# Top-k attention with two expert layers: the scaled excess in fp32 instead of bf16

## The chip, the cores and the metric

The kernel runs on one core of a Trainium2 chip. The metric is the device time of one execution in microseconds; a time is the median of three runs. The engines are named as in the profile: PE (TensorE matmul), PEld (TensorE weight load), DVE (VectorE), ACT (ScalarE), POOL (GpSimd) and SP (SyncE).

## What is computed

Three layers follow one another. Attention keeps, in each row of scores, the 32 largest; a mixture of experts sends each token to one of eight; a dense layer with a hard-swish-like gate ends it.

```
scores = q @ k.T / 8                       # 2 batches, 8 heads, 576 x 576
kth    = 32nd largest of each row
attn   = softmax(scores where scores >= kth) @ v
x      = attn as 1152 tokens x 512
e      = argmax(x @ w_gate); x = gate * (relu(x @ w1[e]) @ w2[e])
h      = x @ w_in; out = (h * clip(h + 3, 0, 6) / 6) @ w_out
```

## The kernel before

The attention stage works on 72 units: 9 tiles of 128 rows times 8 heads, one unit being the 128 x 576 scores of a head for a tile. `in_steps` (L561) runs one step per unit and issues, in each step, pieces of several units that are at different depths. The order inside a step is the string `STEP = "RGLXSCVBTAZFMEQ"` (L36). Each engine works off its own queue in that order, and waits on semaphores for the others.

What happens to one unit, with the lines that matter:

- TensorE makes the scores (L321), ScalarE copies them to SBUF as fp32 (`fetch`, L326).
- **Round one** (L342, DVE): eight MAX8 instructions give the eight largest of each chunk of 72 columns.
- **Excess** (`excess`, L348, POOL): scores minus the eighth value of their chunk, the second operand being broadcast over the 72 columns of a chunk.
- **Cut** (`cut_excess`, L353, ACT): relu of that excess times 2**64, written to the tile `cut`.
- **Drop** (`drop_excess`, L356, POOL): scores minus `cut`, so that all that stood above the eighth value falls far down.
- **Round two** (L360, DVE): one MAX8 over the 576 columns that are left.
- **Merge** (L367, L369, L371, DVE): from the lists of chunk maxima the 32 largest in order.
- **Shift** (L385 on POOL for 200 columns, L390 on ACT for 376) and **below** (L394, ACT): the inputs of the transposes on TensorE (L408, L409), after which come the exponential (L415, ACT), the product with v (L426, PE) and the normalization (L432 to L434, DVE).

In step i POOL's queue holds the excess of unit i, the shift of unit i-3 and the drop of unit i-1, in this order; round two on DVE takes unit i-2, behind round one of unit i+1 and the merge of unit i-3. Every eighth step `judge` adds four small POOL instructions (L377 to L380). After four tiles, and again after eight, DVE also chooses the experts of the finished tiles (`route`, L456, with L466 `dl` and L491 `rd`), and POOL sends their rows with an indirect DMA (L140).

The expert layer and the dense layer come after the attention stage and run for the rest of the span, most of it matmuls.

Of the kernel before, what the change touches and what calls it, by code (L numbers as in the profile page):

```python
# [8 lines left out]
F32 = mybir.dt.float32  # L9
F32R = mybir.dt.float32r  # L10
BF = mybir.dt.bfloat16
# [7 lines left out]
P = 128  # L19
B, H, S, D = 2, 8, 576, 64  # L20
# [37 lines left out]
def topk_attention_moe_ffn_kernel(ctx, tc, qT, kT, vx, vT, wg, w1, w2, w_in, w_out, out, cap):  # L58
# [19 lines left out]
    def forward(fast):  # L78
# [112 lines left out]
        with ExitStack() as actx:  # L191
            big = actx.enter_context(tc.tile_pool(name=of + "big", bufs=1))
            wk = actx.enter_context(tc.tile_pool(name=of + "wk", bufs=2))
# [79 lines left out]
            for i in range(2):  # L273
                u = big.tile([P, 5 * P], F32, name=f"ub{i}")
# [19 lines left out]
            av, cuts = {}, {}  # L294
# [54 lines left out]
                                        op=OP.subtract)  # L349

            def cut_excess(u):
                cuts[u] = wk.tile([P, S], BF, name="cut")
                nc.scalar.activation(cuts[u], st2[u], AF.Relu, scale=PUSH)  # L353

            def drop_excess(u):
# [205 lines left out]
            def in_steps():  # L561
# [15 lines left out]
                def issue(u):  # L577
                    if u % 2 == 0:
                        if u % H == 0 and 2 < u // H + 2 < NT:
# [3 lines left out]
                routes = {}  # L583
                sent = 0
                blocks = {"X": (0, excess), "C": (1, cut_excess), "B": (1, drop_excess), "L": (2, round2), "S": (3, shift),
                          "Z": (3, shift_rest), "M": (3, below), "T": (4, ptr), "E": (4, expo), "A": (5, attv)}
                keep_warm(KW, wm)
# [434 lines left out]
```

## Time and profile before

| What | us |
|---|---|
| Median of three runs | 641.39 (641.07 to 641.99) |
| The profiled execution, its own time | 639.62 |
| Its span, first to last instruction | 637.8 |
| First to last drop (L356 starts) | 10.6 to 232.7 |
| Busy in the span: PE, DVE, ACT, POOL | 609.8, 375.5, 360.3, 311.3 |

The busy times are of the whole span. POOL, DVE and ACT do most of their work in the attention stage, up to about 235 us, and have little to do afterwards, so their shares of the span say little on the attention stage; the stretches of that stage have to be looked at by themselves. A record's duration includes a part that overlaps the next record on the same engine: on POOL some 40 ns.

### The profile page before, as it was taken

The numbers are of one execution on the slowest core, as the hardware profiler recorded it, in microseconds if no ns is written. First come the engines' busy times: TensorE is split into PE (matmuls) and PEld (weight loads), VectorE is DVE, ScalarE is ACT, GpSimd is POOL, SyncE is SP. The second block draws the span as 40 slices with busy tenths as digits, with TensorE's granted clock in tenths as the row PEclk, the third lists the DMA queues.
The fourth block names the chain that finished last, engine by engine and source line by source line (L and its number), as shares of the span: only waits on it lengthen the run. The fifth ranks groups of instructions, "written<-read, shape, count | busy, mean of one in ns | idle before, by whom it ended". The sixth has DMA issues, their size and how long they took to land.

```text
span 637.8 us, 12077 instructions
## 1 busy us (share of the span) xinstructions
PE 609.8 (96%) x4096; PEld 549.2 (86%) x4096; DVE 375.5 (59%) x1765; ACT 360.3 (56%) x687; POOL 311.3 (49%) x380
## 2 busy tenths in 40 slices
PE   8999999999888879999999999999999999999994
PEld 4888889888777767999999999999999999999993
DVE  5999999999999994002333323427665664222220
ACT  5999999989999963121334334336555553242221
POOL 7999999979999953001244222124234322030001
PEclk9999999999999979999999999999999999999998
DMA  8549600100000002885889887422222310020001
GB/s 268 168 134 386 212 17 2 35 2 18 18 18 19 2 1 95 293 290 148 306 264 280 276 308 239 165 64 85 81 85 84 97 34 1 1 99 1 1 1 54
DMA packets 36598, 74.13 MB, mean 116 GB/s; under 512 B 4016, under 2 KB 12464, under 8 KB 36528
## 3 DMA queue, kind: packets, MB, share of 16 engines
q1 hardware_dynamic: 34800, 68.55, 32.7%
q0 software_dynamic: 1728, 4.72, 2.0%
q8 instruction: 34, 0.56, 0.3%
q14 instruction: 36, 0.29, 0.2%
HBM read 63.83 MB, written 9.44 MB: 115 GB/s over the span
## 4 chain that ended last, share of the span: by engine, by line
PE 52%; DVE 24%; issue 15%; POOL 6%; ACT 1%; DMA 1%; DVEq 0%; SPq 0%; POOLq 0%; ACTq 0%
PE hps L819 13%; PE yps L819 13%; PE h L916 8%; PE acc L930 7%; DVE lists L342 7%; DVE lists L360 5%; DVE l L369 4%; DVE tops L371 3%; PE av L426 2%; POOL s L356 2%; PE ps L321 2%; PE pt L408 2%; POOL out_dram L939 1%; PE pt L566 1%; PE mix L443 1%
## 5 line engine op out<-in xcount | busy, mean ns | idle before, releaser
L342 DVE MAX8 lists<-s 128x8 f32<-128x72 f32 x576 | 118.6, 220 | 4.1 <-ACT s L326 4.1
L426 PE MATMUL av<-vt,pts 128*128 128x96 f32 (+1 forms) x800 | 100.5, 275 | 0.0
L916 PE MATMUL h<-x2h,fw 128*128 128x384 f32 x384 | 98.3, 336 | 0.9 <-DVE x2l L837 0.9
L426 PEld LDWEIGHTS av<-vt,pts 128*128 128x128 f32 (+1 forms) x800 | 92.1, 184 | 2.1 <-issue 0.9
L356 POOL TENSOR_TENSOR s<-s,cut 128x576 f32<-128x576 f32 x72 | 92.0, 1277 | 3.6 <-ACT cut L353 3.5
L819 PE MATMUL yps<-hT,wslot 128*128 128x192 f32 x512 | 90.9, 326 | 0.0
L930 PE MATMUL acc<-fw,gh 128*128 128x512 f32 x288 | 89.6, 392 | 0.0
L348 POOL TENSOR_TENSOR s<-s,lists 128x576 f32<-128x576 f32 x72 | 83.6, 1162 | 6.1 <-DVE lists L342 3.8
L408 PE MATMUL pt<-ident,ub 128*128 128x128 f32 x360 | 72.6, 287 | 13.5 <-POOL ub L385 7.9
L819 PE MATMUL hps<-xe,wslot 128*128 128x192 f32 x512 | 84.6, 326 | 0.2 <-DVE sc L184 0.2
L819 PEld LDWEIGHTS hps<-xe,wslot 128*128 128x128 f32 x512 | 83.4, 190 | 0.7 <-issue 0.7
L819 PEld LDWEIGHTS yps<-hT,wslot 128*128 128x128 f32 x512 | 82.1, 190 | 1.2
L408 PEld LDWEIGHTS pt<-ident,ub 128*128 128x128 f32 x360 | 50.8, 141 | 33.6 <-POOL ub L385 16.4
L916 PEld LDWEIGHTS h<-x2h,fw 128*128 128x128 f32 x384 | 70.5, 188 | 5.1 <-DVE x2l L837 1.2
L409 PE MATMUL pt<-drop,lb 128*128 128x128 bf16 x360 | 65.7, 220 | 0.0
L916 PE MATMUL h<-x2l,fw 128*128 128x384 f32 x192 | 64.7, 337 | 0.0
L930 PEld LDWEIGHTS acc<-fw,gh 128*128 128x128 f32 x288 | 53.4, 188 | 9.0
L919 ACT ACTIVATE g<-h,three 128x384 f32<-128x384 f32 x48 | 27.9, 581 | 55.7 <-PE h L916 55.7
L920 DVE SCALAR_TENSOR_TENSOR g<-g,h 128x384 f32<-128x384 f32 x48 | 26.5, 551 | 54.3 <-ACT g L919 53.9
L394 ACT ACTIVATE lb<-s,tops 128x576 bf16<-128x576 f32 x71 | 55.0, 775 | 4.9 <-DVE tops L371 2.8
L924 DVE TENSOR_TENSOR gl<-g,gh 128x384 fp32r<-128x384 f32 x48 | 27.4, 571 | 51.0 <-ACT gh L923 51.0
L923 ACT CAST gh<-g 128x384 fp32r<-128x384 f32 x48 | 24.7, 515 | 57.5 <-PE acc L930 52.9
(393 smaller groups left out, 1057.2 us busy)
## 6 DMA issues: line engine op xcount, KB each, us to landing
wslot<-in_w_dram SPq DMA_DIRECT2D x15, 2048.0 KB, 9.3
raw<-in_w_in_dram SPq DMA_DIRECT2D x16, 512.0 KB, 5.0
raw<-in_w_out_dram SPq DMA_DIRECT2D x16, 512.0 KB, 3.6
xs<-x_tok SPq DMA_DIRECT2D x8, 576.0 KB, 13.1
vt<-in_vx_dram SPq DMA_DIRECT2D x8, 365.0 KB, 3.6
kt<-in_kT_dram SPq DMA_DIRECT2D x8, 288.0 KB, 4.5
vts<-in_vT_dram SPq DMA_DIRECT2D x8, 288.0 KB, 3.8
qt<-in_qT_dram SPq DMA_DIRECT2D x9, 256.0 KB, 4.2
```

Source lines behind the costliest of these rows:

```text
L342: yield lambda c=c: nc.vector.max(lists[t % 2][:, h, c], st[u][:, c * CW:(c + 1) * CW])
L348: nc.gpsimd.tensor_tensor(s2, s, lists[t % 2][:, h, :NCK, KEEP:].to_broadcast([P, NCK, CW]), op=OP.subtract)
L356: nc.gpsimd.tensor_tensor(st2[u], st[u], cuts.pop(u), op=OP.subtract)
L360: nc.vector.max(lists[t % 2][:, h, NCK], st2.pop(u))
L394: nc.scalar.activation(lbufs[u % 2][:, :S], st.pop(u), AF.Relu, bias=tops[t][:, h, TOPK - 1:], scale=-1.0)
L408: nc.tensor.matmul(pt[:, c], ubufs[u % 2][:, cs], ident, is_transpose=True, start=True, stop=False)
L409: nc.tensor.matmul(pt[:, c], lbufs[u % 2][:, cs], drop, start=False, stop=True)
L426: nc.tensor.matmul(av[t, g][rows, h % 4], pts[:, c, cols], vt[b, h // 2][:, at:at + VC], start=c == 0, stop=c == 4)
L819: nc.tensor.matmul(out, wb[:, k], m[:, k], start=first and k == 0, stop=last and k == HP - 1)
L916: nc.tensor.matmul(h2, fw[f][:, 0, a, k * P:(k + 1) * P], (x2h, x2l)[b][:, k, c * CH:(c + 1) * CH], start=n == 0, stop=n == len(ops) - 1)
L919: nc.scalar.activation(g, h2, AF.Relu, bias=three)
L930: nc.tensor.matmul(acc[j], g[a][:, j * P:(j + 1) * P], fw[f][:, 1, b], start=f == 0 and n == 0, stop=f == NF - 1 and n == 2)
```

## The change

The tile `cut` is allocated in fp32 instead of bf16. ScalarE writes fp32 in L353, and POOL's subtraction in L356 reads two fp32 operands of 576 columns instead of one of fp32 and one of bf16. Both kernels hold the same instructions in the same order on every engine, with the same waits; the two buffers of `cut` take twice the space in SBUF.

```diff
             def cut_excess(u):
-                cuts[u] = wk.tile([P, S], BF, name="cut")
+                cuts[u] = wk.tile([P, S], F32, name="cut")
                 nc.scalar.activation(cuts[u], st2[u], AF.Relu, scale=PUSH)
```

## Rows read from the trace of the kernel before

**Rows 1.** Chain that ended last, shares of the span by engine (the page).

```profile
PE 52%; DVE 24%; issue 15%; POOL 6%; ACT 1%; DMA 1%; DVEq 0%; SPq 0%; POOLq 0%; ACTq 0%
```

**Rows 2.** Stretches: length, then busy PE, PEld, DVE, ACT, POOL; clock, DMA, GB/s.

```profile
84.00:132.00 48.00, 47.62 (x418) 41.43 (x416) 47.79 (x314) 46.29 (x80) 47.70 (x57) 1.00 0.06 18
132.00:145.50 13.50, 13.03 (x142) 11.16 (x143) 13.33 (x82) 11.61 (x22) 9.22 (x14) 1.00 0.06 21
145.50:219.00 73.50, 64.95 (x567) 54.67 (x565) 70.93 (x465) 70.89 (x122) 72.65 (x90) 1.00 0.04 13
```

**Rows 3.** Line 356, 145.5 to 219 us: min/median/max ns; who waited (us, times).

```profile
L356 POOL TENSOR_TENSOR s<-s,cut x24: 1265/1272/1279, 145.8 to 217.8; 128x576 f32<-128x576 f32 x24
...
  DVE lists L360: 1.9, 4
```

**Rows 4.** Timeline, drop and round two of unit 66: start us, us, instruction.

```profile
217.75 1.27 POOL L356 TENSOR_TENSOR s<-s,cut 128x576 f32<-128x576 f32 x1
...
219.06 0.76 DVE L360 MAX8 lists<-s 128x8 f32<-128x576 f32 x1
```

**Rows 5.** Groups on POOL: shapes, count, then busy us, mean ns, idle before.

```profile
L356 POOL TENSOR_TENSOR s<-s,cut 128x576 f32<-128x576 f32 x72 | 92.0, 1277 | 3.6 <-ACT cut L353 3.5
L348 POOL TENSOR_TENSOR s<-s,lists 128x576 f32<-128x576 f32 x72 | 83.6, 1162 | 6.1 <-DVE lists L342 3.8 <-DVE lists L360 2.2
L385 POOL TENSOR_TENSOR ub<-tops,s 128x200 f32<-128x200 f32 x70 | 36.1, 516 | 1.8 <-DVE tops L367 1.8
```

**Rows 6.** Lines 717 and 710 on POOL, later stages, columns as in rows 3.

```profile
L717 POOL TENSOR_TENSOR fw<-cm__4505,fw x1: 1257/1257/1257, 315.6 to 315.6; 128x512 fp32r<-128x512 f32 x1
...
L717 POOL TENSOR_TENSOR fw<-cm__5325,fw x1: 1742/1742/1742, 433.0 to 433.0; 128x512 fp32r<-128x512 f32 x1
...
L710 POOL TENSOR_TENSOR cm__4590<-cg__4591,cm__4590 x1: 1257/1257/1257, 320.0 to 320.0; 128x512 int32<-128x512 int32 x1
```

**Rows 7.** Groups on ACT, columns as in rows 5.

```profile
L394 ACT ACTIVATE lb<-s,tops 128x576 bf16<-128x576 f32 x71 | 55.0, 775 | 4.9 <-DVE tops L371 2.8 <-DVE gt L486 0.7 <-DVE rs L432 0.5
...
L353 ACT ACTIVATE cut<-s 128x576 bf16<-128x576 f32 x72 | 49.2, 684 | 1.1 <-POOL s L348 1.1
...
L390 ACT ACTIVATE ub<-s,tops 128x376 f32<-128x376 f32 x70 | 42.5, 607 | 0.2 <-DVE tops L367 0.2
```

**Rows 8.** Line 356, 8 to 85 us; below, what POOL waited for (us, times).

```profile
L356 POOL TENSOR_TENSOR s<-s,cut x25: 1279/1284/1293, 10.6 to 83.1; 128x576 f32<-128x576 f32 x25
...
  ACT cut L353: 2.6, 3
```

**Rows 9.** Timeline, drop and round two of unit 26.

```profile
89.71 1.27 POOL L356 TENSOR_TENSOR s<-s,cut 128x576 f32<-128x576 f32 x1
...
91.31 0.74 DVE L360 MAX8 lists<-s 128x8 f32<-128x576 f32 x1
```

**Rows 10.** Line 356, 85 to 132 us; below, what POOL waited for.

```profile
L356 POOL TENSOR_TENSOR s<-s,cut x16: 1269/1275/1286, 86.0 to 130.7; 128x576 f32<-128x576 f32 x16
...
  ACT cut L353: 0.3, 1
```

**Rows 11.** Timeline around 131 us; in brackets, idle time before and what ended it.

```profile
130.67 1.28 POOL L356 TENSOR_TENSOR s<-s,cut 128x576 f32<-128x576 f32 x1
130.87 1.12 DVE L466 TENSOR_TENSOR dl<-L,mx 128x32 f32<-128x32 f32 x1
...
133.66 1.16 POOL L348 TENSOR_TENSOR s<-s,lists 128x576 f32<-128x576 f32 x1 [1.71 <-DVE lists L360]
```

**Rows 12.** Line 356, 220 to 231 us.

```profile
L356 POOL TENSOR_TENSOR s<-s,cut x4: 1265/1268/1271, 220.6 to 229.1; 128x576 f32<-128x576 f32 x4
```

**Rows 13.** Timeline around 229 us.

```profile
227.50 1.15 POOL L348 TENSOR_TENSOR s<-s,lists 128x576 f32<-128x576 f32 x1
228.53 1.89 DVE L466 TENSOR_TENSOR dl<-L,mx 128x32 f32<-128x32 f32 x1
...
229.10 1.26 POOL L356 TENSOR_TENSOR s<-s,cut 128x576 f32<-128x576 f32 x1
```

## Prediction, written before the changed kernel had run

> **What bounds the kernel now.** I read the chain of waits first: over the whole span it is mostly TensorE, with DVE second and POOL at 6% [rows 1]. TensorE's share belongs to the expert and dense layers. The changed lines run only in the attention stage, so I went on with the busy times by stretch, to see which engine has no idle time left where. From 84 to 132 us TensorE, DVE and POOL are all busy for more than 47.6 of 48 us; from 132 to 145.5 POOL has 4.3 us to spare and DVE 0.2; from 145.5 to 219 POOL is busy for 72.65 of 73.5 us and DVE for 70.93 [rows 2]. So the attention stage has no slack engine, and which one sets the pace changes. What ends last is read from who waits for the drop: from 145.5 to 219 us, 24 drops, round two on DVE waits for it four times, 1.9 us in all [rows 3], and at unit 66 it starts at 219.06, 0.04 us after the drop's end at 219.02 [rows 4]. There POOL is the path: it runs gapless, and any time added to a drop is added to the stage.
>
> **What the change does to one drop.** POOL's subtraction in L356 gets a second operand of 4 instead of 2 bytes per element. No row of before shows it on 576 columns, so I bound it. Two subtractions with a broadcast second operand give a slope: 1162 ns at 576 columns and 516 at 200 [rows 5] make 646/376 = 1.718 ns per column, over a fixed 172 ns. The same line with the bf16 operand: (1277 - 172)/576 = 1.918. Two full operands of 4 bytes exist on 512 columns in a later stage: 1257 ns, whether the result is fp32r or int32 [rows 6]; (1257 - 172)/512 = 2.119. The three slopes, for 0, 2 and 4 bytes of streamed second operand, lie 0.200 and 0.201 apart, so I read POOL's time as going by the bytes it reads. With the slope of 2.119 the fp32 drop takes 172 + 576 x 2.119 = 1393 ns: **116 ns more** than 1277. The bounds: if the 64 columns beyond 512 cost only the broadcast slope, 1257 + 64 x 1.718 = 1367 (90 more); if all of the 1257 scales with the columns, 1414 (137 more). From below, an fp32 operand as cheap as the broadcast one would take 1162 (115 less); that end I keep for a rival, since the 1257 ns on fewer columns already exceed it. From above there is L717 at 1742 ns [rows 6], some 433 us into the span; but the drops of the attention stage stay between 1265 and 1293 ns in all stretches that I looked at [rows 3, 8, 10, 12], so nothing that lengthens L717 there lengthens POOL's work here.
>
> The Trainium skill speaks against this price. GPSIMD Engine Reference, section Performance versus the Vector engine, counts a two-input instruction by elements, about 2.6 cycles for each, because both operands go through one read port, and gives 4497 ns for 2048 fp32 columns; in proportion, as an estimate, 576 columns would take 1265 ns, just what the bf16 drop takes, and the change would cost nothing. The trace does not bear out a count of elements alone, since L348 and L356 have equally many; no run shows the fp32 drop yet.
>
> **ScalarE's side.** L353 writes fp32 instead of bf16. L394 writes 576 bf16 columns in 775 ns and L390, of the same form, 376 fp32 columns in 607 [rows 7]: 168/200 = 0.84 ns per column across the two types, with nothing left for the type. If L353 has 0.84 too, its fixed part is 200 ns and stays. I take 0 for it; bounds of plus or minus 10 ns on 684 are hidden: of the 3.5 us that POOL waits for the cut at all [rows 5], 2.9 lie before 132 us [rows 8, 10], where POOL is not yet the path. The larger tile moves no instruction, no wait and no transfer.
>
> **Where 0.116 us per drop goes.** Step by step along the stage:
>
> (A) 8 to 85 us, units 0 to 24. POOL waits three times for the cut, 2.6 us in 25 drops [rows 8], about 0.87 per eight units, because ScalarE is late there for other reasons. The addition is 8 x 0.116 = 0.93 per eight units. The idle time takes it; 0.06 per eight units is left over, 0.2 us of lateness in all, and round two has 0.33 us to spare even at a tight unit such as 26 (drop ends at 90.98, round two starts at 91.31) [rows 9]. I count **0**.
>
> (B) 85 to 132 us, units 25 to 40. Sixteen drops with one wait of 0.3 us [rows 10]: POOL gets 16 x 0.116 - 0.3 = 1.6 us late. Round two mostly has the slack for that. But at 130.87 DVE runs `dl` (L466), 32 columns in 1.12 us, and it ends with the drop beside it, at 131.99 against 131.95 [rows 11]; at 228.53 the same line takes 1.89 us and ends at 230.42, with the drop at 230.36, having sat through the end of the excess and all of the shift and the drop [rows 13]. I read that `dl` cannot run until POOL pauses. So a drop of unit 40 that ends 1.6 us later lets `dl` go 1.6 us later, and this is on the path: from here to 145.5 us DVE has next to no idle time, while POOL waits 1.71 us for it right behind [rows 2, 11]. I count **1.56**, with 0.1 as the lower bound (`dl` slips in between two POOL instructions, and only the shortfall at unit 26 counts: 2 x 0.116 plus the 0.2 of A, less 0.33).
>
> SBUF — State Buffer of the Trainium skill, section Who interferes with whom, states such an exclusive lock: a DVE instruction with two SBUF inputs and a GpSimd instruction that reads SBUF block one another fully. The trace agrees, with 1.12 and 1.89 us for 32 columns. By that rule B and D count in full and the sum is 4.9 us; without it they fall away and it is 3.0.
>
> (C) 132 to 219 us. Unit 41 adds **0.12** (its drop is followed by another short wait of DVE's in the same place). From unit 43 to 66 POOL is the path [rows 2 to 4]: 24 x 0.116 = **2.78**, all of it, since it is DVE that waits.
>
> (D) 220 to 231 us, units 67 to 70. Round two has slack again, but `dl` at 228.53 ends with the drop of unit 70 [rows 13]: 4 x 0.116 = **0.46** [rows 12]. Behind it the stage ends on DVE, ScalarE and TensorE, and the later layers start later by the whole sum; they are TensorE's and have no idle time to give back [rows 1].
>
> Sum: 0 + 1.56 + 0.12 + 2.78 + 0.46 = 4.9 us. The profiled execution took 639.62 us, of which 637.8 is its span; it would become 644.5. The median of the three runs is 1.8 us higher, 641.39, and the sum is carried over as it is: **646.3 us**.
>
> **The rivals.** (1) `dl` gets the port between two POOL instructions: B shrinks to 0.1 and D to 0, the sum is 3.0 and the time 644.4. For it speaks that there are some 40 ns of handover on POOL; against it that two such handovers, where the excess ended at 228.65 and where the drop began at 229.10, passed without `dl` going on [rows 13]. (2) POOL's time goes by elements and not by bytes: the drop stays at 1277 ns and the time at 641.4. Against it stand the three slopes. (3) Faster: a bf16 operand costs POOL a conversion, and an fp32 operand is as cheap as in L348. Place: the 24 drops from 145.5 us on. Price: each drop 115 ns shorter, 2.8 us for POOL, of which only what DVE waits for can be won, 1.9 us [rows 3], since DVE is the next engine: 639.5. It decides as soon as the fp32 drop is shorter than 1277 ns; against it, two fp32 operands on 512 columns take 1257. (4) POOL's fp32 reads get into the way of DVE as L717 does at 1742 ns: 1742 x 576/512 = 1960 ns, 72 x 0.68 = 49 us, 690 us. Nothing in this stage looks like that.
>
> **How the numbers follow.** Forecast as summed 0.55, rival 1 0.30, rival 2 0.07, rival 3 0.05, rival 4 0.03. The price bounds move the sum: with 90 ns, B to D give 3.7 (2.3 under rival 1, hence 643.7); with 137 ns, B to D give 5.9 and A's leftover 0.7, hence 648.0. Together with the spread of the runs, some 0.3 us on either side, the range is 643.4 to 648.4 and leaves out rivals 2 to 4 and a little of the rest. A difference under 0.2%, 1.3 us, is about what a measurement of this kernel can't tell from none. Faster 0.05, same 0.07, slower 0.88.
>
> **What would show it.** In the profile of the changed kernel: L356 at 1367 to 1414 ns (the price); L353 still at 684; POOL busy for nearly all of the stretch from 85 us on, with its idle time before 85 us gone; more waits of round two for the drop than four and 1.9 us; `dl` near 131 us longer than 1.12 us, by up to 1.6 (step B), and near 230 us longer than 1.89 (step D). If L356 is at 1277 or below, the first step is wrong and so is the sign; if `dl` is short, rival 1 holds.

## The result, and the profile after

The changed kernel takes 647.93 us (median of four runs, 647.64 to 649.42), against 641.69 for the kernel before, measured beside it (641.07 to 642.34): 6.2 us more by the medians; the ratio of the two is 1.0107, with a 95% interval from 1.0095 to 1.0119. The forecast was 4.9 us more, a ratio of 1.0077. The sign came out as forecast, and so, within 0.3 us, did the loss inside the attention stage, 5.2 us; the rest, 1.0 us by the medians and 1.7 by the ratio, lies outside that stage, most of it behind it, where the prediction counted nothing. The profiled execution took 647.75 us, its span 645.9.

The chain that ended last, shares by engine, and three groups of the page of the changed kernel (count, then busy us, mean ns, idle time before and what ended it), which answer to [rows 1, 5]:

```profile
PE 45%; DVE 26%; issue 16%; POOL 8%; ACT 2%; DMA 1%; SPq 0%; POOLq 0%; DVEq 0%; ACTq 0%
...
L356 POOL TENSOR_TENSOR s<-s,cut 128x576 f32<-128x576 f32 x72 | 102.7, 1426 | 0.0
...
L348 POOL TENSOR_TENSOR s<-s,lists 128x576 f32<-128x576 f32 x72 | 85.0, 1182 | 6.9 <-DVE lists L342 4.5
...
L360 DVE MAX8 lists<-s 128x8 f32<-128x576 f32 x72 | 54.0, 752 | 5.4 <-POOL s L356 4.8
```

POOL's share of the chain rose from 6 to 8%. The drop shows a mean of 1426 ns where it was 1277, and POOL never sits idle before it any more: the 3.6 us of [rows 5] are gone. In their place DVE's round two waits 4.8 us for the drop. Of the 149 ns between the two means not all is price. POOL's *records* overlap, and where POOL ran without a pause they grew (last section). The pace is read from start to start of neighbouring records: drop to the next excess, 1239 ns before and 1369 now (over the 57 drops with an excess right behind them). **130 ns per drop** is the price; 116 was forecast, with bounds of 90 and 137.

The same stretches as in [rows 2], columns as there, from the changed kernel:

```profile
84.00:132.00 48.00, 47.61 (x420) 41.78 (x422) 47.51 (x317) 47.20 (x81) 48.00 (x55) 1.00 0.06 18
...
145.50:219.00 73.50, 63.53 (x556) 53.67 (x556) 69.18 (x446) 69.39 (x118) 72.91 (x83) 1.00 0.04 16
```

From 84 to 132 us POOL is busy for all of the 48 us (47.70 before). From 145.5 to 219 it is as full as before, while DVE falls from 70.93 to 69.18 us: it waits. Line 356 by stretch (min/median/max, first and last start, then who waited for it), and line 353 over the span:

```profile
L356 POOL TENSOR_TENSOR s<-s,cut x24: 1397/1405/1415, 148.1 to 222.9; 128x576 f32<-128x576 f32 x24
...
  DVE lists L360: 3.9, 5
```

```profile
L353 ACT ACTIVATE cut<-s x72: 671/684/715, 10.3 to 237.7; 128x576 f32<-128x576 f32 x72
```

For the same 24 drops [rows 3] had 1.9 us of waiting in four places. ScalarE's write of fp32 takes the 684 ns that the write of bf16 took [rows 7].

The place where step B was put, in the timeline of the changed kernel (start us, us, instruction):

```profile
131.59 1.22 POOL L348 TENSOR_TENSOR s<-s,lists 128x576 f32<-128x576 f32 x1
...
132.12 2.58 DVE L466 TENSOR_TENSOR dl<-L,mx 128x32 f32<-128x32 f32 x1
...
132.71 0.58 POOL L385 TENSOR_TENSOR ub<-tops,s 128x200 f32<-128x200 f32 x1
...
133.19 1.46 POOL L356 TENSOR_TENSOR s<-s,cut 128x576 f32<-128x576 f32 x1
```

`dl` takes 2.58 us where it took 1.12 [rows 11], and ends at 134.70, just behind the drop's end at 134.65. It sat through two ends of POOL instructions, at 132.81 and 133.29. The second `dl` takes 2.40 us where it took 1.89 [rows 13]. Between the two, round two of unit 66, which in [rows 4] came 0.04 us behind its drop, now stands waiting for it (in brackets the idle time before, and what ended it):

```profile
222.88 1.41 POOL L356 TENSOR_TENSOR s<-s,cut 128x576 f32<-128x576 f32 x1
...
224.32 0.76 DVE L360 MAX8 lists<-s 128x8 f32<-128x576 f32 x1 [0.61 <-POOL s L356]
```

Behind the stage there is a difference that no step of the forecast speaks of. Two stretches of before and then the same two of the changed kernel, columns as in [rows 2] (the granted clock stands behind the five busy times):

```profile
254.00:258.00 4.00, 3.80 (x23) 3.62 (x23) 0.62 (x7) 0.66 (x2) 2.05 (x4) 1.00 0.72 273
258.00:262.00 4.00, 4.00 (x27) 4.00 (x26) 0.00 (x0) 0.99 (x3) 0.00 (x0) 1.00 0.43 155
```

```profile
254.00:258.00 4.00, 3.35 (x10) 1.95 (x11) 1.15 (x8) 0.72 (x1) 1.09 (x2) 0.58 0.18 70
258.00:262.00 4.00, 3.90 (x13) 2.59 (x12) 1.58 (x8) 0.00 (x0) 1.26 (x2) 0.56 0.33 77
```

In the changed kernel TensorE runs at the lower level, 1.2 of 2.4 GHz, for 6.8 us from 254.7 us on, just where the first expert's matmuls should start (at 254.41 us before, at 261.75 now). Before, it had only one such stretch near the stage's end, 6.8 us from 232.7; the changed kernel has a shorter one there, 3.4 us from 237.6.

### The profile page after: what moved, and what is told of

Read it like the earlier page. It is cut to its first block, busy times and chain, and to the rows that moved or that the text cites. A ratio compares the mean times of both kernels' runs of the same rounds, so it can differ in the third digit from the quotient of the medians.

```text
span 645.9 us, 12077 instructions
## 1 busy us (share of the span) xinstructions
PE 612.4 (95%) x4096; PEld 549.7 (85%) x4096; DVE 378.7 (59%) x1765; ACT 362.4 (56%) x687; POOL 320.5 (50%) x380
## 4 chain that ended last, share of the span: by engine, by line
PE 45%; DVE 26%; issue 16%; POOL 8%; ACT 2%; DMA 1%; SPq 0%; POOLq 0%; DVEq 0%; ACTq 0%
PE hps L819 13%; PE yps L819 13%; PE h L916 8%; DVE lists L342 8%; PE acc L930 7%; DVE lists L360 6%; DVE l L369 5%; POOL s L356 4%; DVE tops L371 3%; POOL out_dram L939 1%; DVE tops L367 1%; POOL s L348 1%; PE xp L153 1%; DVE x_tok L434 1%; POOL ub L385 1%
## 5 line engine op out<-in xcount | busy, mean ns | idle before, releaser
L356 POOL TENSOR_TENSOR s<-s,cut 128x576 f32<-128x576 f32 x72 | 102.7, 1426 | 0.0
L819 PE MATMUL yps<-hT,wslot 128*128 128x192 f32 x512 | 90.9, 326 | 0.0
L348 POOL TENSOR_TENSOR s<-s,lists 128x576 f32<-128x576 f32 x72 | 85.0, 1182 | 6.9 <-DVE lists L342 4.5
L819 PE MATMUL hps<-xe,wslot 128*128 128x192 f32 x512 | 84.6, 326 | 0.1
L819 PEld LDWEIGHTS hps<-xe,wslot 128*128 128x128 f32 x512 | 83.4, 190 | 1.0 <-issue 1.0
L819 PEld LDWEIGHTS yps<-hT,wslot 128*128 128x128 f32 x512 | 82.1, 190 | 1.2
L360 DVE MAX8 lists<-s 128x8 f32<-128x576 f32 x72 | 54.0, 752 | 5.4 <-POOL s L356 4.8
```

What stands on the lines that cost most here:

```text
L348: nc.gpsimd.tensor_tensor(s2, s, lists[t % 2][:, h, :NCK, KEEP:].to_broadcast([P, NCK, CW]), op=OP.subtract)
L356: nc.gpsimd.tensor_tensor(st2[u], st[u], cuts.pop(u), op=OP.subtract)
L360: nc.vector.max(lists[t % 2][:, h, NCK], st2.pop(u))
L819: nc.tensor.matmul(out, wb[:, k], m[:, k], start=first and k == 0, stop=last and k == HP - 1)
```

## The experiments

Three figures from each profile are compared below: the **stage**, from the start of the first excess (L348) to the start of the last round two (L360); the time from the same start to the first matmul of the expert layer (L819); and the stretches in which TensorE was granted half its clock (start, length in us; the last 7 to 9 us of the span, at half clock in every kernel, are left out). All three come from one profiled execution of each kernel, the ratio from all of its executions. e8, with work added behind the stage and one execution of 646.1 us, is read for its timeline alone. The start of the first excess itself moves between 8.3 and 9.9 us from one profile to another, whatever the kernel, so differences are taken from it. Line numbers in the text are those of before.

| kernel | stage | to L819 | half clock | ratio to before |
|---|---|---|---|---|
| before | 227.07 | 246.05 | 232.7, 6.8 | 1 |
| changed | 232.23 | 252.67 | 237.6, 3.4; 254.7, 6.8 | 1.0107 [1.0095, 1.0119] |
| e1_early | 227.11 | 246.23 | 232.7, 6.8 | 0.9999 [0.9990, 1.0008] |
| e2_mid | 228.55 | 247.74 | 235.7, 6.8 | 1.0047 [1.0034, 1.0060] |
| e3_late | 230.78 | 250.02 | 170.4, 3.4; 255.8, 3.4 | 1.0053 [1.0040, 1.0065] |
| e4_pad | 229.91 | 249.81 | 234.3, 6.8; 254.8, 3.4 | 1.0047 [1.0033, 1.0062] |
| e5_view | 231.91 | 249.45 | 236.0, 3.4 | 1.0057 [1.0038, 1.0076] |
| e6_fp8 | 225.42 | 244.52 | 232.4, 6.8 | 0.9975 [0.9959, 0.9991] |
| e7_spool | 228.43 | 248.73 | 233.6, 3.4; 250.7, 6.8 | 1.0010 [0.9996, 1.0024] |
| e9_warm_after | 232.21 | 249.87 | 236.9, 3.4 | 1.0071 [1.0058, 1.0084] |
| e10_warm_before | 227.05 | 246.25 | 232.7, 6.8 | 0.9985 [0.9976, 0.9994] |
| e11_psum_after | 228.51 | 247.16 | none | 1.0073 [1.0055, 1.0091] |
| e12_psum_before | 225.00 | 246.96 | 239.1, 3.4; 252.8, 3.4 | 1.0012 [1.0002, 1.0021] |
| e13_both_before | 224.99 | 245.61 | 236.5, 3.4 | 0.9988 [0.9980, 0.9997] |
| e14_both_after | 228.80 | 249.43 | 169.5, 3.4; 241.2, 3.4 | 1.0061 [1.0044, 1.0078] |
| e15_both_fp8 | 223.83 | 242.85 | none | 0.9975 [0.9961, 0.9989] |

Where its own work is the same, the stage repeats to 0.02 us in three pairs (232.23 and 232.21, 227.07 and 227.05, 225.00 and 224.99) and to 0.28 us in a fourth (228.51 in e11, 228.80 in e14, which has a stretch at half clock inside the stage). The clock does not repeat: which stretches fall differs from kernel to kernel by 3.4 or 6.8 us. So the stage decides between causes here. The whole time follows it only loosely: against before, the ratio gives between 1.2 us less (e5) and 3.2 us more (e11) than the stage.

### Where in the stage the price counts: e1, e2, e3

One part of the units at a time gets the fp32 tile. Theory 1 is the forecast, POOL's time where POOL is the path; theory 2 has every fp32 drop cost the same, wherever it stands.

```diff
-                cuts[u] = wk.tile([P, S], BF, name="cut")
+                cuts[u] = wk.tile([P, S], F32, name="cutw") if u < 25 else wk.tile([P, S], BF, name="cut")
```

(e2: `25 <= u < 43`; e3: `u >= 43`.)

> The cut is fp32 in units 0 to 24 alone, bf16 in the others. Theory 1 (POOL's time per drop, counted only where POOL is the path): the 25 drops take about 1405 instead of 1284 ns, POOL's 2.6 us of waiting before 85 us shrinks to near 0, and the end of the attention stage (last round two) comes 0 to 0.3 us later; time within 0.1% of before. Theory 2 (every fp32 drop costs the same wherever it stands, by ScalarE or by where the larger tile lies): 25/72 of the whole cost of some 6.5 us, 2.3 us slower (0.35%).

> The cut is fp32 in units 25 to 42 alone. Theory 1: the 16 drops up to unit 40 make POOL 16 x 0.13 = 2.1 us late, DVE's small subtraction (dl) near 131 us waits until POOL pauses and takes 2 us more than 1.12, and the end of the attention stage comes 1.8 to 2.2 us later; time 0.3% over before. If the small subtraction does not wait for POOL's pause: 0.1 to 0.4 us. Theory 2: 18/72 of 6.5 us, 1.6 us, and no longer dl.

> The cut is fp32 from unit 43 on. Theory 1: 24 x 0.13 = 3.1 us up to unit 66 and 4 x 0.13 = 0.5 us through the second small subtraction (dl), so the last round two comes 3.4 to 3.7 us later and the time is 0.5 to 0.6% over before, more by up to 1.5 us if TensorE's clock falls a second time behind the attention stage. Theory 2: 29/72 of 6.5 us, 2.6 us.

e1: the 25 early drops became as long as forecast, and nothing followed; the idle time of POOL took it up. Line 356 of e1 (one row for each tile's name), and what POOL still waits for:

```profile
L356 POOL TENSOR_TENSOR s<-s,cut x47: 1264/1277/1304, 86.1 to 232.7; 128x576 f32<-128x576 f32 x47
L356 POOL TENSOR_TENSOR s<-s,cutw x25: 1405/1421/1435, 10.6 to 83.1; 128x576 f32<-128x576 f32 x25
...
  ACT cut L353: 0.6, 1
```

The 2.6 us of waiting of [rows 8] are gone (the 0.6 us left lie behind the 25 drops), and the stage ends 0.04 us later. Step A's zero is shown, and theory 2, which wanted about a third of the loss here, falls. e2 lengthens the stage by 1.48 us, e3 by 3.71; with e1 that makes 5.23, against 5.16 for the whole change. The parts add up. The 1.48 us of e2 are less than the 1.8 to 2.2 expected and by themselves close to theory 2's 1.6; there `dl` decides, which is as long as in the changed kernel:

```profile
132.63 2.61 DVE L466 TENSOR_TENSOR dl<-L,mx 128x32 f32<-128x32 f32 x1
```

### POOL's time alone: e4

The bf16 tile is kept; a small MEMSET on POOL ahead of each drop takes time instead.

```diff
+            pad = big.tile([P, 64], F32, name="pad")
...
             def drop_excess(u):
+                nc.gpsimd.memset(pad, 0.0)
                 nc.gpsimd.tensor_tensor(st2[u], st[u], cuts.pop(u), op=OP.subtract)
```

> The cut stays bf16; instead POOL runs a memset of 128 x 64 fp32 ahead of every drop, so that only POOL's time grows and neither ScalarE's output nor the reading of cut changes. Theory 1: with a memset that adds about 0.1 us to POOL's pace per unit, the stage ends 3.5 to 5 us later, in the same places as in the changed kernel (none before 85 us, some 1.6 at the first dl, the rest from unit 43 on); at another price it scales with it. Theory 2: no cost beyond the waits that POOL's idle time covers, under 1 us.

The MEMSET adds 84 ns to POOL's pace per unit and the stage grows by 2.84 us; 84/130 of the change's 5.16 would be 3.3. The waits of round two appear in the same places: line 356 (here L358) between 146 and 224 us, and who waited for it:

```profile
L358 POOL TENSOR_TENSOR s<-s,cut x25: 1267/1273/1289, 147.2 to 223.9; 128x576 f32<-128x576 f32 x25
...
  DVE lists L362: 3.5, 5
```

The drop itself is as short as before. No fp32 tile, no other write of ScalarE's and no larger buffer is needed for the effect; time on POOL is enough.

### What POOL's price goes by: e5, e6, e8

e5 writes fp32, and reads the upper halves as bf16, two bytes at a stride of four. e6 writes a one-byte float. e8 puts the forms back to back into the expert stage of the kernel before, where POOL is otherwise idle.

```diff
-                nc.gpsimd.tensor_tensor(st2[u], st[u], cuts.pop(u), op=OP.subtract)
+                half = cuts.pop(u).bitcast(BF).rearrange("p (s t) -> p s t", t=2)[:, :, 1]
+                nc.gpsimd.tensor_tensor(st2[u], st[u], half, op=OP.subtract)
```

> ScalarE writes the fp32 cut as in the changed kernel, but POOL reads its upper halves as bf16, 2 bytes at a stride of 4. Theory 1a (POOL's price goes by the span of bytes that it passes over): the drop takes about 1405 ns and the kernel is as slow as the changed one, 1.0% over before. Theory 1b (the price goes by the type that it reads): 1272 to 1280 ns and the time of before, within 0.15%, although ScalarE's output and the larger tile are those of the changed kernel. Theory 2 (ScalarE's output or the tile's place costs): 1.0% over before with a drop of 1280 ns.

```profile
L357 POOL TENSOR_TENSOR s<-s,cut x23: 1392/1404/1411, 147.0 to 217.9; 128x576 f32<-128x576 f32 x23
```

Theory 1a holds: half of the bytes of the fp32 tile cost as much as all of them, and the stage is 4.84 us longer than before. The whole kernel is 0.57% over before and not the 1.0% expected; its profile lacks the stretch at half clock behind the stage. In this run `dl` did get through at the end of the excess. The next DVE instruction with two operands in SBUF, `cand`, waited in its place, to the end of the drop, and the stage is only 0.33 us shorter than that of the changed kernel:

```profile
131.27 0.79 DVE L467 TENSOR_TENSOR dl<-L,mx 128x32 f32<-128x32 f32 x1
...
132.09 1.76 DVE L468 SCALAR_TENSOR_TENSOR cand<-dl,desc 128x32 f32<-128x32 f32 x1
```

```diff
-                cuts[u] = wk.tile([P, S], F32, name="cut")
-                nc.scalar.activation(cuts[u], st2[u], AF.Relu, scale=PUSH)
+                cuts[u] = wk.tile([P, S], mybir.dt.float8e5, name="cut")
+                nc.scalar.activation(cuts[u], st2[u], AF.Relu, scale=2.0 ** 17, saturate=False)
```

> The cut is a one-byte float (e5m2) with a factor of 2**17 in place of 2**64, so that it stays finite; tiny excesses are then pushed down less far. Theory 1 (bytes): by the line through 0, 2 and 4 bytes the drop takes 172 + 576 x 1.82 = 1220 ns, 55 less than bf16; POOL is the path for 24 + 4 units, of which DVE's own work leaves about 1 us to win, so 0.1 to 0.2% faster than before and round two waits for the drop less than 1.9 us from 145 us on. Theory 1b (a narrow type costs a conversion): 1277 ns or more, no gain or slower.

```profile
L356 POOL TENSOR_TENSOR s<-s,cut x26: 1194/1204/1212, 147.2 to 223.5; 128x576 f32<-128x576 f32 x26
...
  DVE lists L360: 1.0, 2
```

The drop takes 68 ns less than with bf16 (1272), the waits of round two fall to 1.0 us, the stage ends 1.65 us earlier, and the kernel is 0.25% faster than before. A narrow type costs no conversion that shows.

```diff
+                    for n, x in enumerate((mb, mg, None, halves)):   # bf16, fp32, broadcast, strided bf16
+                        for i in range(4):
...
+                                g.tensor_tensor(o, mf, x, op=OP.subtract)
```

> The kernel before with 16 more subtractions on POOL in the expert stage, where POOL is idle, back to back, 576 columns: four each with a second operand of bf16, of fp32, of fp32 broadcast over 72 columns, of bf16 at a stride of 4 bytes. DVE runs beside them eight small instructions of 16 columns, two-input and one-input by turns. Theory 1: 1277, 1405, 1162 ns, and for the last one what the kernel with the strided view shows; starts 1239, 1369 and about 1124 ns apart. The small ones with two inputs end only when POOL's run pauses, those with one input take under 200 ns. If prices depend on the attention stage (other engines reading SBUF), all are shorter here.

Timeline of POOL in e8: the last of the four with bf16, then the first with fp32, the last with fp32 ahead of two with a broadcast operand (L817), and the first two with the strided view:

```profile
261.51 1.27 POOL L821 TENSOR_TENSOR mo<-raw,raw 128x576 f32<-128x576 f32 x1
262.75 1.40 POOL L821 TENSOR_TENSOR raw<-raw,raw 128x576 f32<-128x576 f32 x1
...
266.83 1.40 POOL L821 TENSOR_TENSOR mo<-raw,raw 128x576 f32<-128x576 f32 x1
268.19 1.14 POOL L817 TENSOR_TENSOR raw<-raw 128x576 f32<-128x576 f32 x1
269.30 1.15 POOL L817 TENSOR_TENSOR mo<-raw 128x576 f32<-128x576 f32 x1
...
272.62 1.40 POOL L821 TENSOR_TENSOR raw<-raw,raw 128x576 f32<-128x576 f32 x1
273.98 1.40 POOL L821 TENSOR_TENSOR mo<-raw,raw 128x576 f32<-128x576 f32 x1
```

From start to start they take about 1107, 1234 and 1361 ns for 0, 2 and 4 bytes per element of the second operand, that is 127 ns for each two bytes; the strided view counts as four. The line gives 1170 ns for one byte; e6's pace is 1172. Equal counts of elements have four prices here, so the rule of the Trainium skill (GPSIMD Engine Reference, section Performance versus the Vector engine), a fixed number of cycles for each element of a two-input instruction, does not hold across operand types in these runs. The small DVE instructions refuted a part of the expectation: one-input ones did not keep under 200 ns, one taking 1.68 us beside the MEMSETs that come first and another 0.80 us beside a subtraction, and a two-input one ended at the end of a single POOL instruction, 0.56 us after its start. So neither "two inputs only" nor "not before POOL pauses" holds everywhere.

### POOL's time given back: e7

```diff
-SPOOL = 200
+SPOOL = 124
```

> The changed kernel with 124 instead of 200 columns of the shift on POOL (76 columns move to ScalarE). POOL gets 76 x 1.718 = 131 ns per unit back, what the fp32 drop took; ScalarE gets 76 x 0.84 = 64 ns more. Theory 1: POOL's pace is that of before, round two waits for the drop 2 to 3 us in all as before, and the time is 0 to 0.3% over before, the rest being ScalarE's, busy 70.9 of 73.5 us between 145.5 and 219. If POOL's time is not the cause, it stays 1.0% over before.

The changed kernel with less of the shift on POOL is 0.1% over before, where 1.07% stood; the stage is 1.36 us longer than before instead of 5.16. Line 356 from 146 to 224 us and who waited for it:

```profile
L356 POOL TENSOR_TENSOR s<-s,cut x25: 1397/1405/1415, 147.2 to 222.1; 128x576 f32<-128x576 f32 x25
...
  DVE lists L360: 2.0, 4
```

The drops are as long as in the changed kernel, and round two waits as little as in [rows 3]. It is the sum on POOL that counts, not the drop.

### The clock behind the stage: e9, e10

Seven dummy matmuls are put where TensorE waits for the last tokens' routing, into the changed kernel and into the one before.

```diff
                 interleave(gate(t))
+                warm(4)
...
                     *most(tot)])
+                warm(3)
                 x_rows(banks)
```

> The changed kernel with seven more dummy matmuls on TensorE behind the attention stage (four while DVE computes the last gates, three before the rows come back). If the second stretch at half clock (254.7 us, 6.8 us long) comes of TensorE's idle time there, it goes, and some 3 us come back: 644.5 to 646. If it comes of what TensorE did before, it stays and the time is 647.5 to 649.

> The kernel before with the same seven dummy matmuls. Its profile has no second stretch at half clock, so nothing is to be won: within 0.2% of before, slower by at most the 1.7 us that the matmuls take.

The changed kernel won 2.3 us by the medians (645.67), and its second stretch at half clock is gone. The stretches of e9 that answer to those shown of before and after:

```profile
254.00:258.00 4.00, 3.73 (x20) 2.54 (x19) 1.59 (x9) 0.35 (x1) 1.09 (x2) 1.00 0.17 66
258.00:262.00 4.00, 3.79 (x23) 3.46 (x22) 0.78 (x7) 0.66 (x2) 2.05 (x4) 1.00 0.74 244
```

Before won 0.15%, a little more than the nothing that was expected; the profile of one execution does not show where. With the same dummy matmuls in both, the two stand 645.67 - 640.48 = 5.2 us apart. That this is the difference of their stages, 5.16, is in part chance: in the profiles the first expert matmul comes only 3.62 us later, the first stretch at half clock being 3.4 us long in e9 and 6.8 in e10, and another 0.95 us lie behind it.

### Is `dl` held up by POOL, and who pays: e11 to e14

Three small tiles of the routing (`mx`, `dl`, `cm`) are put into PSUM, so that `dl` and the two-input instructions behind it read only one operand from SBUF.

```diff
-                mx, dl, el, cand, cm, gt, a, pr, d = (
-                    r("mx", 1), r("dl"), r("el"), r("cand"), r("cm", 1), r("gt", 1), r("ra"), r("pr", 1),
-                    r("rd", 1))
+                el, cand, gt, a, pr, d = r("el"), r("cand"), r("gt", 1), r("ra"), r("pr", 1), r("rd", 1)
...
+                pt_ = temp([P, 2 * NT, E + 2], "pos_p")
+                pp, dl, mx, cm = pt_[:, :NT, :E], pt_[:, NT:NT + n, :E], pt_[:, NT:NT + n, E:E + 1], pt_[:, NT:NT + n, E + 1:]
```

> The changed kernel with three small tiles of the routing (mx, dl, cm) in PSUM, so that DVE's two-input instructions there read one operand from SBUF and one from PSUM. If two SBUF inputs are what keeps dl waiting beside POOL, dl takes about 0.2 us instead of 2.4 to 2.6. Theory 1a (dl hands POOL's lateness to DVE, step B as forecast): with dl short, round two of unit 40 no longer pays for it and 1.5 to 2.5 us come back against the changed kernel. Theory 1b (dl is only the place where the wait shows, since round two of unit 40, next in DVE's order, needs the drop that ends at 134.65 anyway): it starts at 134.7 instead of 135.53 and only some 0.8 us, with 0.6 more at the second dl, come back, as many as before wins by the same edit; the difference between the two stays 0.8 to 1.0%.

> The kernel before with the same three tiles in PSUM. dl takes about 0.2 us instead of 1.12 and 1.89; round two of unit 40 starts at the end of its drop, 132.0, instead of 132.82, and behind the second dl some 0.6 us are won: 1.0 to 1.5 us in all, 0.15 to 0.25% faster than before. If dl keeps its length, two SBUF inputs are not the reason, and the time is that of before.

The place of step B in e11, timeline:

```profile
132.33 1.25 POOL L348 TENSOR_TENSOR s<-s,lists 128x576 f32<-128x576 f32 x1
...
132.69 0.17 DVE L465 TENSOR_REDUCE pos_p<-L 128x4 f32<-128x32 f32 x1
...
132.89 0.20 DVE L466 TENSOR_TENSOR pos_p<-L,pos_p 128x32 f32<-128x32 f32 x1
...
133.12 0.19 DVE L467 SCALAR_TENSOR_TENSOR cand<-pos_p,desc 128x32 f32<-128x32 f32 x1
...
133.91 0.75 DVE L360 MAX8 lists<-s 128x8 f32<-128x576 f32 x1
```

`dl` takes 0.20 us in the middle of POOL's work, where it took 2.58. Its second operand in SBUF is what held it. The Trainium skill says so (SBUF — State Buffer, section Who interferes with whom): a DVE instruction with at most one SBUF input, outside the two-port modes, does not contend with GpSimd; these rows agree. The same section counts `tensor_scalar` among the instructions that can enter such a mode. In e11 a one-input TENSOR_SCALAR (L486 there) takes 0.91 us and ends with the drop beside it, at 237.0, and 0.16 us later on, with POOL idle.

Theory 1a holds, and 1b falls with a reading of mine: round two behind `dl` takes unit 39 and not 40, as the two expectations have it, and the drop of unit 39 had ended at 131.69 in the changed kernel; the one that ends at 134.65 is unit 40's. The changed kernel's stage shrinks by 3.72 us, that of before by 2.07, more than either expectation; the two stand 3.51 us apart instead of 5.16. The total of e12 did not follow its stage: it fell on two half-clock stretches, 252.8 us among them, and is 0.1% slower. e11 and e12 alone can't be compared by their times, since the clock differs; so both edits, the tiles in PSUM and the dummy matmuls, were put together:

> The kernel before with the routing tiles in PSUM and the seven dummy matmuls. The edit in PSUM ended the attention stage 2.1 us earlier and lost it again to two stretches at half clock; without the second of them 1 to 2 us should be left: 0.15 to 0.35% faster than before. If the clock takes it in any case, the time is that of before.

> The changed kernel with both edits. Theory 1 (only POOL's pace from unit 43 on is left, 24 + 4 units x 0.130): 3.0 to 3.7 us, 0.45 to 0.6%, over e13, and the stage ends 3.5 us later than in it. If the forecast's step B were POOL's own lateness and not handed on by dl, the two stand 5.2 us apart as before.

The stages stand 3.80 us apart, the medians 644.92 - 640.56 = 4.4, the ratios 0.73%, all three more than expected. e13 is 0.12% faster than before, a little less than the 0.15 to 0.35% expected. So with `dl` free, 1.4 of the 5.16 us go (1.65 by e11 and e12). What is left: round two of unit 43 comes 0.75 us later in e14 than in e13, and the other 3.05 us are added from there to the stage's end, where 27 drops at 0.130 would make 3.5.

### Faster than both: e15

The one-byte cut of e6 with both edits:

> The kernel with the one-byte cut (factor 2**17) and both edits. POOL's drop takes 68 ns less than with bf16; by theory 1 POOL is the path for some 24 units, so up to 1.6 us less than e13, 0.4 to 0.6% faster than before, with waits of round two for the drop near 0. If DVE is the path once dl is short, it equals e13.

Its stage is the shortest of all, 223.83 us, its time 0.25% less than before, not the 0.4 to 0.6% expected and not more than e6 has by itself. The executions of both spread over 4 us, from 637 to 641.5, with the clock: those under 638 us have a mean granted clock of 0.995, those over 640 us 0.988 to 0.991. Both are faster than the two kernels of this case. The smaller factor is a change of what is computed: excesses are pushed down by 2**17 instead of 2**64 times their size.

## Why the prediction came out as it did

The step that failed is the last sentence of step D: behind the stage the later layers were to start later by the whole sum, and no more. That put the difference behind the stage at nothing. The runs show a second stretch at half clock there (6.8 us from 254.7 us); without it, in e9, the changed kernel is 2.3 us faster. Two terms of the sum were mis-sized beside it: the price of a drop, and what of step B is left when `dl` is free. The mechanism of the stage, POOL's time where POOL is the path, was right. That 647.93 us lies inside the range is in part luck: the range was made from the bounds of the price and the spread of the runs, and nothing in it stands for the clock.

- **Price of a drop: 116 forecast, 130 measured.** The idea (the time goes by bytes) was right, and the bounds of 90 and 137 held. The size failed where a slope was made from two fp32 operands on 512 columns of a later stage with the fixed part of another form [rows 5, 6]. e8, with all forms at 576 columns, gives 127 for two bytes, and e1 to e3 give it in place.
- **ScalarE: 0 forecast, 0 measured** (684 ns in both).
- **A, units 0 to 24: 0 forecast, 0.04 measured** in e1. POOL's idle time took most of the 25 x 0.130 us; the drop of unit 24 ends 0.23 us later in the changed kernel, counted from the first excess, where the forecast left over 0.2.
- **B, units 25 to 42: 1.56 + 0.12 forecast.** In the changed kernel the drop of unit 40 and `dl` end together, 1.99 and 1.98 us later than before, counted from the first excess; round two of unit 42 starts 1.63 us later. e2 alone keeps 1.48 to the stage's end. The mechanism is shown by e11: `dl` without a second SBUF input takes 0.20 us. It isn't all of the term: between e14 and e13, where `dl` is free, round two of unit 43 is still 0.75 us late. Under rival 1 the forecast counted 0.1 for step B, which is too little.
- **C, units 43 to 66: 2.78 forecast, 2.92 measured** (counted from the first excess, round two of unit 66, waiting for its drop, starts 4.55 us later than before, that of unit 42 1.63). The 24 drops at 0.130 would make 3.12, which is what e3 shows at unit 66; in the changed kernel 0.2 of it was hidden, and the two errors cancel in part.
- **D, units 67 to 70: 0.46 forecast, 0.52 at the end of the second `dl`, 0.62 at the stage's end.** e3, which has C and D alone, measures 3.71 for both.
- **Stage: 4.9 forecast, 5.16 measured.**
- **Outside the stage: 0 forecast, 1.0 measured by the medians, 1.7 by the ratio.** The first expert matmul starts 6.63 us later, counted from the first excess. The 1.46 us between that and the stage lie where the clock differs: the shorter first stretch at half clock gives time back, the second takes more, and in e9, without the second, the first expert matmul is 3.82 us late instead of 6.63. In the profile another 0.8 us come behind the first expert matmul; in e1 to e9, leaving out e8 with its added work, the work from there on takes between 0.2 us less and 1.2 us more than in before, and what sets that isn't settled. With the 0.7 us by which the first excess itself starts later this makes the 8.1 us between the two profiled spans; the profiled execution of before was about 2 us below its median.
- **The rivals.** (1) `dl` slipping through: not in the changed kernel; in e5 it does, and `cand` waits in its place. (2) Price by elements, and (3) an fp32 operand cheaper than bf16: refuted by 1405 ns and by e8. (4) Contention as at L717: not seen; the drops stay between 1388 and 1477 ns.

The signs named ahead were there: the drop's median of 1405 ns from 146 us on, inside 1367 to 1414, POOL's idle time gone, seven waits of round two in place of five (4.8 us in all), `dl` longer by 1.46 and 0.51 us.

What stays open: why the clock falls behind the stage, between 250 and 256 us, in the changed kernel, e3, e4, e7, e8 and e12, and not in e2, nor in e5, whose stage is within 0.33 us of the changed kernel's. TensorE was busy for 2.53 of the 4 us from 252 to 256 in the changed kernel (the last 1.3 of them at half clock already) and for 2.78 of those from 248 to 252 in before, where the clock held. e9 shows that more work for TensorE there removes the stretch, and not what tips it.

## What to carry to other kernels

Cost a POOL instruction by the bytes that its operands span as well as by its columns, and take the price from start to start of neighbouring records at the same width. Then ask, stage by stage, whether POOL has idle time: the same 130 ns were worth nothing in the first 25 units and all of it in the last 28 that count (e1 and e3). A stage that ends a few microseconds later also shifts where TensorE idles, so the clock behind it belongs in the range of the forecast.

## What the runs showed that was not expected

**POOL's records grow while it never pauses.** The excess (L348) in the changed kernel, from 10 to 40, 100 to 134 and 146 to 219 us:

```profile
L348 POOL TENSOR_TENSOR s<-s,lists x12: 1157/1159/1171, 9.1 to 39.8; 128x576 f32<-128x576 f32 x12
```

```profile
L348 POOL TENSOR_TENSOR s<-s,lists x11: 1200/1220/1231, 101.0 to 131.6; 128x576 f32<-128x576 f32 x11
```

```profile
L348 POOL TENSOR_TENSOR s<-s,lists x23: 1154/1157/1182, 146.5 to 217.4; 128x576 f32<-128x576 f32 x23
```

The instruction did not change. From 40 us on, with POOL busy without a gap, the records of all its instructions lengthen little by little, by some 80 ns at most whatever their size (the shift from 511 to 589 ns), and are short again after POOL's pause behind `dl`. The pace does not change: excess to shift takes 1121 to 1127 ns from start to start throughout. So a mean of durations (1426) overstates the price; the median behind a pause (1405) and the pace (1369 against 1239) don't.

**Half a tile costs as much as all of it**: bf16 read at a stride of four bytes takes 1404 ns, as fp32 does, and one byte per element takes 1204.

**`dl` with one operand in PSUM** takes 0.20 us in place of 1.12 to 2.58, and the three tiles in PSUM shorten the stage of the kernel before by 2.07 us; the time of the whole kernel hardly changes (1.0012 in e12, 0.9988 in e13), with other stretches at half clock in each.
